# Gated attention with a token and channel mixer: two mirrored key groups in batch 0, and weight loads that wait for the newest square

## The chip, the cores and the metric

The kernel runs on one core of a Trainium2 chip. The metric is the device time of one execution in microseconds (us); several runs are summarised by their median. One execution was also taken with the hardware profiler, and its trace is what the views below are read from. "The span" is the time from the first to the last instruction in that trace.

## The reference

For each of 8 batches, with S = 3008 rows, 256 columns and keys of 64 columns, all inputs in float32:

```python
scores = z @ z.T / S                     # 3008 x 3008, symmetric
attn   = maximum(scores, 0) ** 2
x      = u * (attn @ v)                  # gated attention
h      = maximum(x.T @ w_tok1, 0) @ w_tok2
y      = x + h.T                         # token mixer, 256 tokens wide
out    = y + maximum(y @ w_ch1, 0) @ w_ch2   # channel mixer, 1536 wide
```

The query and the key are the same z, so the score matrix is symmetric: the block of query block q against key group g is the transpose of the block of query block g against key group q.

## The kernel before, in words

**Tiling.** The rows are cut into six query blocks of 512 rows (the last one has 448) and into six key groups of four 128-row tiles (the last group, number 5, ends with a half tile). A block (b, q, g) is batch b, query block q, key group g. It is made in two units: two score matmuls side by side in the two halves of the array's rows (L440), a relu from PSUM into a bfloat16 tile `at` (ScalarE, L478), and a square in place (VectorE, L486). Then PE multiplies the squared block with `v` into the sums `acc` (L677, also in two row halves at once; L593 for the first query block). When all six groups are summed, the result is added up, gated with the transposed `u` (tile `uT`) and kept as `xT`, which a transposing DMA turns into `x_sb` for the mixer.

**Mirrors.** In batches 1 to 7 only blocks with g >= q are computed. A block with g > q is written in a second layout, and when it is squared, a transposing DMA issued on SP (`flip`, its DMA at L546) writes its mirror, block (b, g, q), into a tile `fl`; such an `at` tile has two uses, its own matmuls and the DMA. In batch 0 every block is computed and none is mirrored, because `MIRROR = NQ` makes `direct_block` true for all of them. There are 6 buffers for `at` and 15 for `fl`; the six `v` tiles of batch 0 lie in `fl` buffers too, until the last query block has used them.

**Who decides the order.** All instructions are placed by a planner in the kernel's own code, which runs when the program is built: it keeps an estimated time for PE (`pe[0]`) and for ScalarE, VectorE and SP, and chooses the next piece of work from buffers and results that it estimates to be ready. `key_order` gives the order in which blocks of a query block are made and used; `units` is the list of score units of the whole run. On the chip, each engine works through its list in order and waits on semaphores.

**Loads.** All loads of `v`, `z`, `u` and the weights are issued on GpSimd's queue (POOL), with a cast to bfloat16. In batch 0 they are hung on the count of key groups that PE has begun (`at_group`): the list `items` (L1626) spreads six `v` loads of batch 1, six of `w_tok1`, six of `w_tok2`, four of `w_ch1` and `w_ch2` and two of `u` for batch 1 over groups 7 to 33. That is only an order in POOL's list: no instruction of POOL waits for the group's work, so POOL issues as soon as one of its eight DMA semaphores is free again. From batch 1 on, loads are asked for at least 4 us of planned time apart, and each is preceded by `after(recent[0])` (L121), a copy of one column of the newest square (or of a later stage's newest tile) into a scrap tile `mark`, so that POOL waits for that work.

**SP's queue** holds all transposing DMAs in one order: `uT`, `zT` of the next batch, `x_sb`, `fl`, and `at` blocks on the diagonal, and the stores of the output.

The mixer of a batch is woven into the attention of the next one. That of batch 0 begins after the first query block of batch 1.

Of the kernel before, what the change touches and what calls it, by code (L numbers as in the profile page):

```python
# [57 lines left out]
def kernel(  # L58
# [22 lines left out]
    NQ = (S + QW - 1) // QW  # L81
    NG = KT // GK
# [30 lines left out]
    def rows_of(ap, c):  # L113

        n = full_tiles[c]
        return ap[c * QW:c * QW + n * P, :].rearrange("(p t) d -> p t d", t=n)

    def last_rows(ap):
        return ap[(KT - 1) * P:, :]

    def after(column):  # L121

        nc.gpsimd.tensor_copy(mark[:column.shape[0], :1], column)
# [77 lines left out]
    def load_v(b, c):  # L201
        if b == 0:

            vt = sb.tile([P, GK, D], BF16, tag="fl", name="v_sb", bufs=ROOM["fl"])
            live["fl"] += 1
            fl_free.pop(0)
        else:
            vt = sb.tile([P, GK, D], BF16, tag="v", name="v_sb", bufs=ROOM["v"])
            live["v"] += 1
        n = full_tiles[c]  # L210
        nc.gpsimd.dma_start(out=vt[:, :n, :], in_=rows_of(v[b], c))
        if n < GK:
            for r in range(2):
                nc.gpsimd.dma_start(
                    out=vt[r * TAIL:(r + 1) * TAIL, n, :], in_=last_rows(v[b]))
        vs[b, c] = vt
        v_in[b, c] = Done(pe[0] + 9.0 if b > 1 else 0.0)
        loading(LOAD)
# [20 lines left out]
    def load_w_tok1(c):  # L239
        n = full_tiles[c]  # L240
        nc.gpsimd.dma_start(
            out=w_tok1_sb[:, c * GK:c * GK + n, :], in_=rows_of(moe_w_tok1, c))
        if n < GK:
            nc.gpsimd.memset(w_tok1_sb[TAIL:, KT - 1, :], 0.0)
            nc.gpsimd.dma_start(
                out=w_tok1_sb[:TAIL, KT - 1, :], in_=last_rows(moe_w_tok1))
        loading(LOAD)
# [20 lines left out]

    WHOLE, MIRROR = 1, NQ
    zTs, vs, urs, uTs, xTs, xs = {}, {}, {}, {}, {}, {}
    v_in = {}
    attn = {}

    def direct_block(b, q, g):

        return g >= q or (b == 0 and g < MIRROR)

    def flips(b, q, g):  # L280

        return g > q and not direct_block(b, g, q)
# [3 lines left out]
    def key_order(b, q):  # L286

        direct = [g for g in range(LAST) if direct_block(b, q, g)]
        flipped = [g for g in range(LAST) if not direct_block(b, q, g)]
        first = (b, q) == (0, 0)  # L290
        if first:
            direct = FIRST[:-1]
        made = direct + [LAST] if first else direct[:1] + [LAST] + direct[1:]
        order = []
        while direct or flipped:
            order += direct[:1] + flipped[:1]
            del direct[:1], flipped[:1]
        order.insert(LAST if first else 2, LAST)
        return made, order
# [13 lines left out]
    def loading(us):  # L313
        loads[0] = max(loads[0], pe[0] + 1.0) + us
# [9 lines left out]
    ROOM = {"at": 6, "fl": 15, "xT": 9, "v": NG, "us": 3, "res": RES}  # L324
# [86 lines left out]
    def can_score(first_unit, most):  # L411

        n, at = 0, live["at"]
        for (b, q, g), pr in units[first_unit:first_unit + most]:
            if (b, q) not in turned or (b, g) not in turned:
                break
            at += pr == 0
            if at > ROOM["at"]:
                break
            n += 1  # L420
        return n
# [62 lines left out]
    def square(unit, view, t):  # L484
        (b, q, g), pr = unit
        nc.vector.tensor_mul(view, view, view)  # L486
        if (b, q, g) in early:
            for e in early[b, q, g][2 * pr:2 * pr + 2]:
                e.t = t
            if pr == 0:  # L490
                blocks[b, q, g] = (
                    Done(t), ats[b, q, g].rearrange("p (i w) -> p i w", w=QW), "at", [1])
            else:
                ats.pop((b, q, g))
            return
        if pr < GK // 2 - 1:
            return
        at = ats.pop((b, q, g))
        uses = [1]
        if flips(b, q, g):  # L500
            uses[0] = 2
            attn = at.rearrange("p (j i s) -> p i j s", i=GK, s=P)
            done = push("sp", t, 2.2, 6.5, lambda t: flip(b, q, g, at, uses, done),
                        frees=fl_free,
                        room=lambda: has_room(("fl",)) and flips_fit(b) and (
                            b < 2 or q or
                            x_done[divmod(b * NQ + q - 1, NQ)].t is not None))
        else:
            attn = at.rearrange("p (i w) -> p i w", w=QW)
        blocks[b, q, g] = (Done(t), attn, "at", uses)  # L510
        recent[0] = at[:, :1]
# [24 lines left out]
    def flips_fit(b):  # L536

        n = live["fl"] - live["mix"]
        before_mixer = b < 2 and goal[0] < (0, 0)
        return n < (MIRRORS if before_mixer else AHEAD if in_mixer[0] else ROOM["fl"])  # L540

# [148 lines left out]
    def next_half(t):  # L690

        blk = cur[0]
        if blk is None:
            return FAR, None
        if blk.whole:
            return next_whole(t)
        if blk.g is not None:
            g, dh, tiles = blk.steps[blk.half]
            at = t if blk.acc[dh or 0] is not None else slot_ready(t)
            return max(at, block_ready(blk, g)), g  # L700
        at = t if blk.acc[0] is not None else slot_ready(t)
        return next_group(blk, at)
# [780 lines left out]
    def at_group(n, f):  # L1483
        fetch.setdefault(n, []).append(f)
# [3 lines left out]
    recent = [None]  # L1488
# [131 lines left out]
    W_LATER = 4  # L1620

    def ask_w_tok2(c):
        load_w_tok2(c)
        tok2_done[c].t = pe[0] + 10.0

    items = [lambda c=c: load_v(1, c) for c in vorder]  # L1626
    items += [lambda c=c: load_w_tok1(c) for c in range(NG)]
    items += [lambda c=c: ask_w_tok2(c) for c in range(NG)]
    items += [lambda part=part: ask_w_ch(part) for part in range(4)]
    items += [lambda m=m: load_u(m // NQ, m % NQ) for m in (NQ, NQ + 1)]  # L1630
    for k, item in enumerate(items):
        at_group(NG + 1 + k * (NQ * NG - 2 * NG + W_LATER) // len(items), item)

    fill(7, bank_pair(0, "wp")[:, 0, :])

# [32 lines left out]
    while cur[0] is not None or heads or tails:  # L1668
# [3 lines left out]
        ta, g = next_half(t)  # L1672
# [15 lines left out]
        n = can_score(done_units, most)  # L1688
# [118 lines left out]
```

## Time and profile before

| | us |
|---|---|
| median of 3 runs | 1116.61 (1116.57 to 1119.4) |
| the profiled execution, its own time | 1118.43 |
| its span | 1116.6 |
| PE busy | 1110.1 |
| VectorE busy | 760.8 |
| ScalarE busy | 671.0 |
| GpSimd busy | 152.6 |
| attention of batch 0 after its first query block, by PE's timeline | from 26.9 to 89.9 |
| mixer of batch 0, first matmul of `a_ps` | 101.51 |

The granted clock of TensorE is 1.000 throughout. Busy time is the time in which an engine had an instruction in work; matmuls overlap one another in the array, so their single durations are longer than the step from one to the next. A DMA is shown with the time that its issue took on the queue of its engine, and with the time from issue to landing.

### The profile page before, as it was taken

To read this page: it belongs to the slowest core of one execution; us is meant where nothing else is said; L and a number is where in the kernel's file an instruction comes from. 1 tells how busy PE (TensorE), PEld (TensorE's weight loads), DVE (VectorE), ACT (ScalarE), POOL (GpSimd) and SP (SyncE) were. 2 spreads that over 40 slices of the span, in tenths; PEclk is the share of its full clock that TensorE was granted. 3 is DMA by queue.
4 is the path that set the end of the run, shared out by engine and by line. 5 is a ranking of instruction groups with operands and counts; after the bars stand their busy time and mean duration, and the time that the engine had idled before them with its cause. 6 is when DMAs were issued, how large, how long until landed. Compare 5 with 4: busy or idle time off the path is not lost.

```text
span 1116.6 us, 26566 instructions
## 1 busy us (share of the span) xinstructions
PE 1110.1 (99%) x10788; PEld 672.0 (60%) x10788; DVE 760.8 (68%) x1593; ACT 671.0 (60%) x846; POOL 152.6 (14%) x387
## 2 busy tenths in 40 slices
PE   9999999999999999999999999999999999999998
PEld 3555655666447665676545765567654576545776
DVE  6887766676756867568666676566756677655676
ACT  7996676545755467555665456664666636743464
POOL 5401100221002210022100221003210021000000
PEclk9999999999999999999999999999999999999999
DMA  9999587998849988599795997869888697574222
GB/s 177 184 167 156 123 168 132 179 182 149 165 111 191 173 134 172 107 204 168 146 170 104 204 152 151 171 101 217 143 150 162 121 202 145 119 153 81 68 64 80
DMA packets 473004, 165.98 MB, mean 149 GB/s; under 512 B 435824, under 2 KB 451504, under 8 KB 472880
## 3 DMA queue, kind: packets, MB, share of 16 engines
q1 hardware_dynamic: 445024, 131.57, 60.3%
q0 software_dynamic: 27344, 32.32, 20.9%
q8 instruction: 84, 1.38, 0.6%
q10 hardware_dynamic: 512, 0.38, 0.1%
q14 instruction: 40, 0.33, 0.1%
HBM read 65.40 MB, written 24.64 MB: 81 GB/s over the span
## 4 chain that ended last, share of the span: by engine, by line
PE 99%; DMA 0%; DVE 0%; SPq 0%; issue 0%
PE acc L677 42%; PE hp L977 22%; PE f L1096 18%; PE sc L440 7%; PE a_ps L900 4%; PE h_ps L927 4%; PE f L1209 1%; PE first_acc L593 1%; PE op L1255 0%; DMA zf<-in_z_dram 0%; PE first_acc L198 0%; PE zp L177 0%; DVE zr L171 0%; PE up L1589 0%; DVE res L1287 0%; SPq L162 0%
## 5 line engine op out<-in xcount | busy, mean ns | idle before, releaser
L1024 ACT ACTIVATE h2pre<-hp 128x1024 bf16<-128x1024 f32 (+1 forms) x287 | 283.3, 1005 | 226.6 <-PE hp L977 218.1
L677 PEld LDWEIGHTS <-v_sb 64*128 64x128 bf16 x4418 | 235.4, 94 | 223.1 <-issue 1.1
L677 PE MATMUL acc<-at,v_sb 64*128 64x512 bf16 (+1 forms) x2738 | 337.3, 374 | 0.0
L478 ACT ACTIVATE at<-sc 128x1024 bf16<-128x1024 f32 (+1 forms) x284 | 279.7, 1029 | 72.3 <-PE sc L440 66.9
L977 PE MATMUL hp<-xT,w_ch_sb 128*128 128x512 bf16 (+1 forms) x1152 | 281.7, 375 | 0.0
L486 DVE TENSOR_TENSOR at<-at 128x1024 bf16<-128x1024 bf16 (+1 forms) x284 | 194.0, 687 | 122.3 <-ACT at L478 120.4
L1096 PEld LDWEIGHTS <-h2pre 128*128 128x128 bf16 x3654 | 225.0, 98 | 55.3 <-issue 2.6
L677 PE MATMUL acc<-fl,v_sb 64*128 64x512 bf16 (+1 forms) x1680 | 192.2, 367 | 0.0
L1096 PE MATMUL f<-w_sums,h2pre 128*128 128x128 bf16 x2088 | 184.4, 219 | 0.0
L977 PEld LDWEIGHTS <-w_ch_sb 128*128 128x128 bf16 x1152 | 104.3, 98 | 82.1 <-issue 0.8
L440 PE MATMUL sc<-zT 64*128 64x512 bf16 (+1 forms) x732 | 132.3, 360 | 0.0
L1096 PE MATMUL f<-w_ch_sb,h2pre 128*128 128x128 bf16 x1566 | 128.5, 219 | 0.0
L811 DVE TENSOR_TENSOR cp<-acc,cp 128x512 f32<-128x512 f32 (+1 forms) x94 | 63.5, 676 | 59.9 <-ACT cp L805 59.1
L805 ACT COPY cp<-acc 128x512 f32<-128x512 f32 (+1 forms) x91 | 53.0, 583 | 81.9 <-PE acc L677 81.4
L466 ACT ACTIVATE at<-sc 128x512 bf16<-128x512 f32 (+3 forms) x164 | 59.1, 452 | 35.5 <-PE sc L440 30.4
L1049 DVE TENSOR_TENSOR h2pre<-h2pre 128x512 bf16<-128x512 bf16 (+1 forms) x141 | 56.3, 400 | 18.7 <-PE f L1096 17.8
L440 PEld LDWEIGHTS <-zT 64*128 64x128 bf16 x732 | 40.2, 94 | 41.5 <-issue 3.8
L1170 DVE TENSOR_TENSOR res<-f,res 128x512 f32<-128x512 f32 (+1 forms) x47 | 30.6, 651 | 49.7 <-PE f L1096 49.7
L1051 DVE TENSOR_TENSOR h2pre<-h2pre 128x512 bf16<-128x512 bf16 (+1 forms) x141 | 57.1, 405 | 9.4 <-DVE h2pre L1050 0.5
L936 DVE TENSOR_TENSOR xT<-xT,h_ps 128x1024 bf16<-128x1024 bf16 (+1 forms) x48 | 55.8, 1171 | 11.2 <-PE h_ps L927 11.2
L835 DVE TENSOR_TENSOR xT<-cp,uT 128x512 bf16<-128x512 f32 (+1 forms) x94 | 62.5, 664 | 1.2
L518 DVE TENSOR_TENSOR at<-at 128x512 bf16<-128x512 bf16 (+3 forms) x164 | 43.9, 320 | 25.0 <-ACT at L466 23.9
(80 smaller groups left out, 623.7 us busy)
## 6 DMA issues: line engine op xcount, KB each, us to landing
out_dram<-res SPq DMA_DIRECT2D x80, 256.0 KB, 2.4
v_sb<-in_v_dram POOLq DMA_DIRECT2D x40, 256.0 KB, 4.8
ur<-in_u_dram POOLq DMA_DIRECT2D x40, 256.0 KB, 5.2
out_dram<-res SPq DMA_DIRECT2D x24, 128.0 KB, 2.0
w_tok_sb<-in_moe_w_tok_dram POOLq DMA_DIRECT2D x10, 256.0 KB, 10.2
zs<-in_z_dram POOLq DMA_DIRECT2D x35, 64.0 KB, 3.9
at<-at SPq DMA_TRANSPOSE x123, 2.4
fl<-at SPq DMA_TRANSPOSE x105, 4.6
```

Source lines behind the costliest of these rows:

```text
L440: nc.tensor.matmul(sc[:, r, c0:c1], zT[h, k:k + P], zT[h, m + c0:m + c1], start=True, stop=True)
L466: nc.scalar.activation(a3[:, i, c0:c1], sc[:, r, c0:c1], ACT.Relu, scale=inv_S)
L478: nc.scalar.activation(view, sv, ACT.Relu, scale=inv_S)
L486: nc.vector.tensor_mul(view, view, view)
L677: nc.tensor.matmul(o, vs[blk.b, g][rows, i, dh * P:(dh + 1) * P], rhs, start=(dh, h) not in blk.begun, stop=stop, skip_group_check=True)
L811: nc.vector.tensor_add(cp[:, :W], acc[:, 0, :W], cp[:, :W])
L835: nc.vector.tensor_mul(xT[:, dh, :full * P].rearrange("p (t s) -> p t s", s=P), acc[:, :full * P].rearrange("p (t s) -> p t s", s=P), uT[: ...
L977: nc.tensor.matmul(hp[:, r, :W], w_ch1_sb[:, dc, cc * P:(cc + 1) * P], xT[:, dc, :W], start=(dc == 0), stop=(dc == DT - 1))
L1024: nc.scalar.activation(h2[:, :, :W], hp[:, :, :W], ACT.Relu)
L1049: (3, lambda: nc.vector.tensor_sub(a11, a11, a21)),
L1051: (2, lambda: nc.vector.tensor_sub(a22, a22, a11)),
L1096: banked(nc.tensor.matmul(to[:, j, :], lhs[:, j * P:(j + 1) * P], rhs, start=m in (1, 2) and c2 == 0 and j == 0, stop=c2 == CHT // 2 - 1, ...
```

## The change

Two things change, both in batch 0. The key groups 3 and 4 of the last query block are no longer computed: blocks (0, 3, 5) and (0, 4, 5) are written in the mirror layout and their mirrors come by DMA. With that, the order in which query block 5 uses its groups goes from 0, 1, 5, 2, 3, 4 to 0, 3, 5, 1, 4, 2, and the order in which it makes them from 0, 5, 1, 2, 3, 4 to 0, 5, 1, 2. And every load of `items` behind the six `v` loads (the 16 loads of weights and the two of `u`) is preceded on POOL by `after(recent[0])`.

```diff
-    WHOLE, MIRROR = 1, NQ
+    WHOLE = 1
+    FLIPPED = ((5, 3), (5, 4))
...
     def direct_block(b, q, g):
 
-        return g >= q or (b == 0 and g < MIRROR)
+        return g >= q or (b == 0 and (q, g) not in FLIPPED)
...
         n = live["fl"] - live["mix"]
+        if b == 0:
+            return n < ROOM["fl"]
         before_mixer = b < 2 and goal[0] < (0, 0)
         return n < (MIRRORS if before_mixer else AHEAD if in_mixer[0] else ROOM["fl"])
...
+    def paced(item):
+        after(recent[0])
+        item()
+
...
     for k, item in enumerate(items):
-        at_group(NG + 1 + k * (NQ * NG - 2 * NG + W_LATER) // len(items), item)
+        at_group(NG + 1 + k * (NQ * NG - 2 * NG + W_LATER) // len(items),
+                 (lambda item=item: paced(item)) if k >= NG else item)
```

## The prediction

> **What bounds the kernel now.** I read the page's busy times and chain first, then PE by stretches of ten microseconds, then PE's timeline around the last query block of batch 0, and last the DMA issues of two short stages.
>
> The page says that PE is busy almost all the time and that the chain of work that ended last consists of PE:
>
> ```profile
> PE 1110.1 (99%) x10788; PEld 672.0 (60%) x10788; DVE 760.8 (68%) x1593; ACT 671.0 (60%) x846; POOL 152.6 (14%) x387
> ...
> PE 99%; DMA 0%; DVE 0%; SPq 0%; issue 0%
> ```
>
> The table by stretches shows the stage that the change touches (columns: stretch, its length, then busy time and count for PE, weight loads, VectorE, ScalarE, POOL, then PE's clock, DMA share, GB/s):
>
> ```profile
> 30.00:40.00 10.00, 10.00 (x96) 5.35 (x94) 7.86 (x12) 10.00 (x12) 4.41 (x10) 1.00 1.21 198
> 70.00:80.00 10.00, 10.00 (x102) 5.57 (x98) 8.38 (x15) 8.97 (x12) 0.75 (x2) 1.00 1.27 137
> 80.00:90.00 10.00, 10.00 (x106) 6.02 (x104) 7.58 (x13) 9.31 (x12) 0.00 (x0) 1.00 0.60 119
> ```
>
> PE has no gap there. Busy time alone would not prove it, as single matmuls overlap, so I check the step from one instruction to the next in PE's timeline (start, length, line, what, count). It also shows the work that the change removes:
>
> ```profile
> 77.67 0.37 PE L440 MATMUL sc<-zT 64*128 64x448 bf16 x2
> 77.86 0.94 PE L677 MATMUL acc<-at,v_sb 64*128 64x448 bf16 x8
> 78.61 0.37 PE L440 MATMUL sc<-zT 64*128 64x448 bf16 x2
> 78.80 1.69 PE L677 MATMUL acc<-at,v_sb 64*128 64x448 bf16 x16
> ```
>
> Eight matmuls, four pairs, take 78.61 - 77.86 = 0.75 us, 0.19 a pair, and a score pair the same 0.19 (77.67 to 77.86); the pairs follow each other at one step whatever they belong to. So the time is the sum of PE's steps: a removed pair is worth its step, and everything else counts only when it makes PE wait.
>
> The Trainium skill ("Trainium Kernel Development and Optimization", Performance Expectations) calls matmul busy time a bad metric for the distance to the limit and wants the use of the array counted. Had only the 99% been there, the gain could be anything from nothing to the whole sum; the constant step agrees with the full sum, so I keep it.
>
> **What the change removes from PE.** Blocks (0,5,3) and (0,5,4) have two score units each, so 4 pairs of 448 columns: 4 x 0.19 = 0.76 us. Their matmuls with `v` stay, now read from `fl`; the groups have the same mean there as from `at` at full width (367 ns against 374 on the page), so no change. ScalarE loses 4 relus and VectorE 4 squares, worth nothing because PE does not wait for either in this stage.
>
> **What it adds on SP.** Two transposes of an `at` tile, 128 x 2048 values of 2 bytes = 0.52 MB each. They have much time before block 5 uses them: (0,3,5) is squared at 49.0, (0,4,5) at 61.8, and query block 5 starts on PE at 77.86. The tighter limit is the `at` buffer: six buffers go round, so the sixth block after it writes the same one. Counting two score pairs a block back from the first 448-wide pair at 69.47, block (0,3,5) has its scores at 45.72 and 46.59, block (0,4,5) at 58.46 and 59.32, block (0,5,5) at 71.14. VectorE's timeline gives the squares of the second units:
>
> ```profile
> 48.34 0.69 DVE L486 TENSOR_TENSOR at<-at 128x1024 bf16<-128x1024 bf16 x1 [0.23 <-ACT at L478]
> ...
> 61.07 0.69 DVE L486 TENSOR_TENSOR at<-at 128x1024 bf16<-128x1024 bf16 x1 [0.22 <-ACT at L478]
> ```
>
> They end at 49.03 and 61.76. ScalarE starts a relu about 0.6 us after its scores (0.45 for block 5), so the buffers are written again at 59.07 and 71.59. **Each mirror has some 10.0 and 9.8 us to land**; what lands later delays a relu, then a PSUM bank, then PE.
>
> How long does a mirror take? The two stages of the trace of before lie far apart. While POOL's loads run (27 to 53 us; size, then median us from issue to landing):
>
> ```profile
> w_tok_sb<-in_moe_w_tok_dram POOLq DMA_DIRECT2D x10, 256.0 KB, 10.2
> w_ch_sb<-in_moe_w_ch_dram POOLq DMA_DIRECT2D x4, 384.0 KB, 15.0
> ...
> zT<-zs SPq DMA_TRANSPOSE x3, 20.6
> ...
> x_sb<-xT SPq DMA_TRANSPOSE x1, 17.2
> uT<-ur SPq DMA_TRANSPOSE x1, 18.9
> ```
>
> and when none runs (87 to 94 us):
>
> ```profile
> fl<-at SPq DMA_TRANSPOSE x2, 4.3
> ...
> x_sb<-xT SPq DMA_TRANSPOSE x1, 3.0
> ```
>
> So the lower end is 4.3 us, the upper 17.2 to 20.6. Which one holds depends on the other half of the change.
>
> **What the waits do.** In before, POOL issues the weights as fast as its semaphores allow:
>
> ```profile
> 28.72 1.60 POOL L241 DMA_DIRECT2D w_tok_sb<-in_moe_w_tok_dram  x3
> ...
> 51.46 0.83 POOL L263 DMA_DIRECT2D w_ch_sb<-in_moe_w_ch_dram  x1 [0.74 <-DMA w_tok_sb<-in_moe_w_tok_dram]
> ```
>
> The first lands at about 28.7 + 10.2 = 38.9, the last at 51.5 + 15.0 = 66.5. With the waits, item k goes to group 7 + 28k/24, so the 16 weight loads to groups 14 to 31. Groups take (77.86 - 26.90) / 24 = 2.12 us (PE's timeline: query block 1 starts at 26.90, block 5 at 77.86). That is 44 to 80 us. POOL's issues at 33.91, 35.33 and 36.82 each waited for one of the last loads of `v` and `u`; so from 36.8 to 44 no load would run, and SP can catch up: the `zT` transposes, which held it until 62.7 in before, have room ahead of the first mirror.
>
> In before the loads from 37 to 66.5 take 29 us for 17 items (one of them `u`), 1.7 us each; 16 x 1.7 = 27 us of the 38 from 44 to 82, a share of 0.71. A transpose moves 0.61 MB in 26 us beside loads (the queue totals for 27 to 53 us), 0.023 MB/us, and about 0.28 MB/us alone (GB/s row of 87 to 94). The mean is 0.29 x 0.28 + 0.71 x 0.023 = 0.098 MB/us, so a mirror needs 5.4 us, plus 4.3 - 0.52/0.28 = 2.4 fixed: **an estimate of 7.8 us, under the 9.8 it has**. I take no stall, and keep 4.3 and 20.6 as ends. In SP's queue only `uT` and `x_sb` (0.26 MB each) can stand ahead of a mirror.
>
> What else stands behind a waiting mark on POOL: the loads of `u` block 5 (now about 55, turned about 62, needed for the gate after 90), `u` of batch 1 (about 82 to 85, landing 5.2 us later by the page; turned at 88.5 and 95.65 in before), and a memset. Who waits for the weights: `w_tok1`, issued by 55, is used at 101.51; `w_tok2` by 70, at 106.96; `w_ch`, issued by 80 to 82 and landing 15.0 later at most, 97, is summed by VectorE at 96.31 in before and used by PE at 109.57. The cover is 12 us on PE; without it each microsecond late is one lost.
>
> The 18 marks take 0.18 us each on POOL (the median of the rows at L123), 3.3 us in all. In before, 8 squares overlap a mark and take 0.690 us on average, as the 202 others do, and VectorE idles 1.6 to 2.4 us in each ten of the table above: I take nothing; without that cover they would cost VectorE their 3.3 us.
>
> The Trainium skill ("SBUF — State Buffer", Who interferes with whom) speaks against them: a VectorE instruction with two SBUF inputs and a GpSimd instruction that reads SBUF lock each other out of a port. By it the marks could hold VectorE for as long as they last; the squares of this trace show no such loss.
>
> **The sum.** 1118.43 - 0.76 = 1117.67 for the profiled execution, whose time stands 1.82 above the median; the span 1116.6 - 0.76 = 1115.8. For the median: 1116.61 - 0.76 = **1115.85 us**, -0.07%. A measurement of this kernel can tell about 0.3% from no change, 3.35 us; this lies inside.
>
> **Rivals.**
>
> First, **the mirrors land late** (slower). They wait in SP's queue, or loads come in clumps: groups 16 and 17, 18 and 19, 22 and 23 are begun together. For: the 17.2 to 20.6 above. Against: the loads are spread. It decides from 10.0 us on; past 0.76 us of lateness in total the change loses, past 4.1 us by over 0.3%. At 17.2 each: (17.2 - 10.0) + (17.2 - 9.8) = 14.6, 1130.4 us; at 12 each 4.2, 1120.0. Chance 0.16: half of it a small loss up to 4.1 us (up to 1119.9), half above.
>
> Second, **the weights come too late** for the mixer: needs 12 us beyond 97; if `w_ch` took 30 us, 3 us, 1118.9. Chance 0.03, 0.01 of it above the bound.
>
> Third, **the waits don't spread the loads**, because the newest square in POOL's list is already done when POOL gets there. Then the mirrors fall under the first rival, with 17.2: 1130.4. Chance 0.02.
>
> Fourth, **the planner's order shifts** after block 5: batch 1 starts four units earlier, and the 0.2 us that PE loses at 90.8 (the score pair at 90.77 is followed after 0.4 instead of 0.22) may go or others come: 1115.3 to 1117. Chance 0.07.
>
> Fifth, **ScalarE bounded the stage after all** (10.00 of 10 in 30:40): then 4 relus of 0.93 us (the 128x896 form) go, 3.7 us, 1112.9. PE's even step speaks against it. Chance 0.02.
>
> **How the numbers follow.** The forecast has 0.70. Faster by over 0.3%: 0.02. Slower: 0.08 + 0.01 + 0.02 = 0.11. Within: 0.87. The range goes from 1115.3, the lower end of the fourth rival, to 1118.6, which takes in the smaller stalls (up to 2.7 us over the forecast); what lies outside is the 0.11 above the bound, the upper part of the small stalls and the fifth rival, some 0.17.
>
> **What would show it.** Right: 8 score matmuls at L440 fewer; `fl` transposes 105 + 2; landings of `zT` and `x_sb` in 27 to 53 us down from 17 to 20 to under 8; PE 10.00 in each ten from 30 to 90. Wrong: ScalarE waiting for a DMA at 59 or 72, with PE below 10.00 there, or PE waiting before `a_ps`, `h_ps` or `hp` of batch 0 for a weight.

## The result, and the profile after

| | before | after |
|---|---|---|
| median of 6 runs each, us | 1116.66 (1115.78 to 1119.4) | 1131.2 (1128.93 to 1142.24) |
| the profiled execution, us | 1118.43, span 1116.6 | 1131.22, span 1129.4 |

The ratio is 1.0136, 95% interval 1.0111 to 1.0161: slower by 14.5 us. The forecast was 1115.85; the first rival (mirrors land late) had named 1130.4. In all comparisons below, single runs that stand over 1.5% above the fastest run of the same kernel are left out of the ratio; where that matters, all times are listed.

The page of after answers to the lines shown of before: busy times, the chain that ended last, the score matmuls, and TensorE's clock in 40 slices of 28 us.

```profile
PE 1110.7 (98%) x10780; PEld 672.1 (60%) x10780; DVE 759.2 (67%) x1589; ACT 667.6 (59%) x842; POOL 157.6 (14%) x405
...
PEclk9979999999999999999999999999999999999999
...
PE 97%; DMA 3%; DVE 0%; ACT 0%; issue 0%; ACTq 0%
...
L441 PE MATMUL sc<-zT 64*128 64x512 bf16 (+1 forms) x724 | 130.3, 359 | 12.2 <-ACT at L479 12.2
```

The work went as the diff says: 8 score matmuls fewer (724, before 732), 4 relus and 4 squares fewer. But DMA now stands in the chain with 3%, the score matmuls carry 12.2 us of idle time, and the third slice has a lower clock. The table by stretches finds the place (PE, weight loads, VectorE, ScalarE, POOL, PE's clock, DMA share, GB/s):

```profile
50.00:60.00 10.00, 9.62 (x90) 5.09 (x87) 7.80 (x13) 7.98 (x9) 4.39 (x10) 1.00 1.27 139
60.00:70.00 10.00, 0.00 (x0) 0.00 (x0) 0.00 (x0) 0.00 (x0) 0.00 (x0) 0.69 1.45 91
70.00:80.00 10.00, 8.17 (x52) 3.61 (x53) 5.81 (x10) 6.06 (x7) 1.70 (x4) 0.63 1.01 173
80.00:90.00 10.00, 10.00 (x98) 5.38 (x96) 7.88 (x14) 8.93 (x11) 4.82 (x10) 1.00 0.74 113
```

For ten microseconds nothing computes at all; only the DMA engines are busy. The chain of work between 40 and 80 us (start, length, what) says which transfer that is:

```profile
47.10 0.75 PE acc L680 x7
47.85 22.82 DMA fl<-at
...
70.75 1.03 ACT at L479
...
71.83 0.61 PE sc L441 x2
```

It is the first new mirror, issued on SP at 47.85. It lands 22.8 us later, at 70.67, and 0.08 us after that ScalarE begins the relu that writes the same `at` buffer again. ScalarE had been ready since 70.75 - 12.35 = 58.40, as its own timeline shows (the bracket is the idle time and what ended it):

```profile
70.75 2.85 ACT L479 ACTIVATE at<-sc 128x1024 bf16<-128x1024 f32 x3 [12.35 <-DMA fl<-at]
```

So the mirror had 58.40 - 47.85 = 10.55 us from its issue and took 22.8. (The prediction's 10.0 us count from the end of the block's second square. VectorE's timeline has that square at 45.66 for 0.69 us here, so counted like this the mirror had 58.40 - 46.35 = 12.05.) PE stopped when its PSUM banks were full, and came back at half speed:

```profile
59.01 0.61 PE L680 MATMUL acc<-at,v_sb 64*128 64x512 bf16 x4
71.83 0.61 PE L441 MATMUL sc<-zT 64*128 64x512 bf16 x2 [12.21 <-ACT at L479]
72.21 1.94 PE L680 MATMUL acc<-at,v_sb 64*128 64x512 bf16 x8
73.92 0.66 PE L441 MATMUL sc<-zT 64*128 64x512 bf16 x2
74.34 3.44 PE L680 MATMUL acc<-at,v_sb 64*128 64x512 bf16 x16
77.61 0.39 PE L441 MATMUL sc<-zT 64*128 64x512 bf16 x2
```

From 72.21 to 73.92 four pairs of 512 columns take 1.71, 0.43 each; from 77.61 on (0.39 for two that overlap, the next group at 77.82) the step is 0.21 again. From 71.83 to 77.61 fourteen pairs take 5.78 us where 14 x 0.215 = 3.0 would do: 2.8 us lost behind the pause.

**Where the time went.** The spans differ by 12.8 us. From the first `acc` matmul to the first `a_ps` after had 88.79 us and before 74.61, 14.18 more; the parts are 12.4 of pause (59.24, start of the last pair, to 71.83, less one step) + 2.8 of slow steps - 0.76 of removed pairs = 14.4. The profiled execution of before had begun its first `acc` matmul 2.69 us later (26.90 against 24.21); PE's list is the same in both up to there, so this is not counted to the change. From the first `a_ps` of batch 0 to that of batch 1 after has 1.09 more; 1.0 of it is a wait of PE for an `at` transpose that took 5.9 us beside a load of `u` (182 to 188 us). The rest differs by 0.2.

**What ran beside the mirror.** DMA issues of after in 47 to 49 us (size, median us to landing):

```profile
w_tok_sb<-in_moe_w_tok_dram POOLq DMA_DIRECT2D x1, 256.0 KB, 9.9
w_tok_sb<-in_moe_w_tok_dram POOLq DMA_DIRECT2D x1, 192.0 KB, 10.3
uT<-ur SPq DMA_TRANSPOSE x1, 11.5
fl<-at SPq DMA_TRANSPOSE x1, 22.8
```

and the DMA engines in the ten microseconds of standstill, with packets, megabytes and share of the 16 engines for SP's transposes (q1) and POOL's loads (q0):

```profile
GB/s 42 79 59 57 43 56 51 40 72 52 43 57 52 52 48 61 53 49 42 58 71 71 147 138 140 89 124 113 122 129 114 159 156 182 193 157 168 113 102 83
DMA packets 1827, 0.91 MB, mean 91 GB/s; under 512 B 1228, under 2 KB 1827, under 8 KB 1827
...
q1 hardware_dynamic: 1197, 0.30, 84.5%
q0 software_dynamic: 630, 0.61, 60.5%
```

The crowded stage of before shows how slow this is. There both kinds of traffic ran together too (27 to 53 us):

```profile
DMA packets 5605, 4.91 MB, mean 189 GB/s; under 512 B 2780, under 2 KB 4321, under 8 KB 5601
...
q0 software_dynamic: 3147, 4.26, 96.5%
q1 hardware_dynamic: 2454, 0.61, 18.8%
```

That is 164 GB/s of loads and 23 of transposes. In the standstill both together move 91, and 53 in its first five microseconds. Loads with hardly a transpose beside them moved 192 (81 to 83 us of the fifth experiment), transposes alone 280 to 290. A transposing packet carries 0.30 MB / 1197 = 250 bytes. On average it took 0.845 x 160 us / 1197 = 113 ns in the standstill, 0.188 x 416 / 2454 = 32 ns in the crowded stage of before, and 18 ns where no load runs (the fences of the fifth experiment below: 0.783 x 24 / 1068). So this is not the crowded stage of before again, but a worse one.

### The profile page after: what moved, and what is told of

Same layout as the page of the kernel before. It is cut to its first block, busy times and chain, and to the rows that moved or that the text cites. A ratio compares the mean times of both kernels' runs of the same rounds, so it can differ in the third digit from the quotient of the medians.

```text
span 1129.4 us, 26576 instructions
## 1 busy us (share of the span) xinstructions
PE 1110.7 (98%) x10780; PEld 672.1 (60%) x10780; DVE 759.2 (67%) x1589; ACT 667.6 (59%) x842; POOL 157.6 (14%) x405
## 4 chain that ended last, share of the span: by engine, by line
PE 97%; DMA 3%; DVE 0%; ACT 0%; issue 0%; ACTq 0%
PE acc L680 40%; PE hp L980 22%; PE f L1099 18%; PE sc L441 6%; PE a_ps L903 4%; PE h_ps L930 4%; DMA fl<-at 2%; PE f L1212 1%; PE first_acc L596 1%; DMA at<-at 1%; PE op L1258 0%; PE wp L198 0%; DVE cp L814 0%; PE first_acc L198 0%; ACT at L479 0%
## 5 line engine op out<-in xcount | busy, mean ns | idle before, releaser
L479 ACT ACTIVATE at<-sc 128x1024 bf16<-128x1024 f32 (+1 forms) x280 | 275.7, 1031 | 83.1 <-PE sc L441 64.8
L487 DVE TENSOR_TENSOR at<-at 128x1024 bf16<-128x1024 bf16 (+1 forms) x280 | 191.5, 688 | 133.2 <-ACT at L479 130.6
L680 PE MATMUL acc<-fl,v_sb 64*128 64x512 bf16 (+1 forms) x1712 | 196.3, 367 | 0.0
L441 PE MATMUL sc<-zT 64*128 64x512 bf16 (+1 forms) x724 | 130.3, 359 | 12.2 <-ACT at L479 12.2
L123 POOL CAST mark<-at 128x1 f32<-128x1 bf16 x30 | 8.8, 293 | 438.2 <-DVE at L487 438.2
L939 DVE TENSOR_TENSOR xT<-xT,h_ps 128x1024 bf16<-128x1024 bf16 (+1 forms) x48 | 55.8, 1171 | 11.5 <-PE h_ps L930 11.5
```

Of the source, the lines that this page charges most:

```text
L441: nc.tensor.matmul(sc[:, r, c0:c1], zT[h, k:k + P], zT[h, m + c0:m + c1], start=True, stop=True)
L479: nc.scalar.activation(view, sv, ACT.Relu, scale=inv_S)
L680: nc.tensor.matmul(o, vs[blk.b, g][rows, i, dh * P:(dh + 1) * P], rhs, start=(dh, h) not in blk.begun, stop=stop, skip_group_check=True)
```

## The experiments

The theory after this result: a mirror lands late because weight loads are in flight beside it, and the two kinds of traffic slow each other. The rivals: SP's queue holds it up, the buffer count alone decides, the waits themselves hold something, or the cost lies in another part of the change than the mirrors. Line numbers of `kernel.py` shift by a few where lines were added.

### One part alone

**The waits without the mirrors.**

```diff
-    FLIPPED = ((5, 3), (5, 4))
+    FLIPPED = ()
```

> The waits on the newest square stay, no block is mirrored (the list of mirrored pairs is empty). Theory (the loss is a mirror that lands too late while loads run, and holds its at buffer): no mirror, no stall; PE's step unbroken from 30 to 90 us, 1116.6 us within 1; uT and x_sb still land in 10 to 17 us between 44 and 70 us, since the loads still run there. Rival (the waits themselves or the later weights cost the time): over 1120 us, with PE waiting before 110 us.

Measured: 1131.09, 1117.16, 1135.31, 1116.84, 1134.56, 1116.82 us, before 1116.93 beside it; ratio 1.0023 (0.9976 to 1.0069). Batch 0 has no pause, as the theory says. But three of six runs took 14 to 18 us more, and the one of them that was profiled shows why: the waits moved the tail of the loads from 66.5 us to about 100, under the first mirror of batch 1. In before that mirror was issued at 87.09 and landed in 4.3. Its landing, and the waits between 80 and 112 us (total, times, longest):

```profile
fl<-at SPq DMA_TRANSPOSE x1, 19.7
```

```profile
ACT at L479 <- DMA fl<-at: 12.8, 1, 12.8
...
PE sc L441 <- ACT at L479: 11.5, 1, 11.5
```

So half of the runs meet the theory's time; the other half meet the rival's, over 1120 us, and the profiled one also its PE wait before 110 us. The later weights can cost the time by themselves. The wait is again one for a mirror that lands beside loads, but it is a mirror that the change does not touch.

**The mirrors without the waits.**

```diff
-                 (lambda item=item: paced(item)) if k >= NG else item)
+                 item)
```

> The two mirrors stay, the weight loads do not wait. Theory: block (0,3,5)'s mirror is squared at 49 us in the middle of the loads, stands behind zT on SP and lands after 65 us or later, so ScalarE and PE wait over 6 us for the at buffer, (0,4,5) adds some: 1122 to 1145 us. Rival (the waits cost the time): no stall, 1115.9 us.

Measured: 1134.92, 1132.45, 1133.14, 1150.83; ratio 1.0139 (1.0108 to 1.017). Here SP is still busy with `zT` until 62.7, so the first mirror is issued only at 71.19. By then the loads are all but done and it lands quickly, but it is 18.0 us late. Landing (71 to 73 us), and waits (60 to 110 us):

```profile
fl<-at SPq DMA_TRANSPOSE x1, 4.8
```

```profile
ACT at L479 <- DMA fl<-at: 18.0, 1, 18.0
PE sc L441 <- ACT at L479: 17.8, 1, 17.8
```

So the mirrors cost this much with or without waits, in two ways: with loads in the DMA engines, the transposes ahead of the mirror hold SP and delay its issue, or the mirror itself lands late.

**One mirror at a time, waits kept.** `FLIPPED = ((5, 4),)`, then `FLIPPED = ((5, 3),)`.

> The waits stay, only key group 4 of the last query block is mirrored (its mirror landed in 6.7 us in the changed kernel, but behind a stall in which POOL issued nothing). Theory: without that stall it is squared at about 62 us beside the loads of w_tok2 and lands in 12 to 20 us against 9.8 allowed: a stall of 2 to 10 us, 1118 to 1127 us. Rival (only the first mirror has a problem, because it stands behind uT on SP): lands under 8 us, no stall, 1116.2 us.

Measured: 1145.13, 1144.2, 1116.14, 1116.17, all outside the 1118 to 1127 of the theory. The profiled run is the first: the mirror, issued at 63.75 behind a `uT` beside `w_tok2` and `w_ch`, needs 34.9 us (DMA issues of 63 to 65 us):

```profile
uT<-ur SPq DMA_TRANSPOSE x1, 16.6
fl<-at SPq DMA_TRANSPOSE x1, 34.9
```

The two short runs stand 0.8 below the median beside them (1116.93), where one mirror should save 2 pairs x 0.19 = 0.4; the scatter of before (1116.07 to 1117 for most runs) covers the difference. They were not profiled, but a mirror that is late by more than its cover would show in their time. So the same order of loads can leave a mirror in time, or cost 28 us.

> The waits as in the change, only key group 3 mirrored. Theory (the first mirror is squared in the middle of the w_tok1 loads and lands some 22 us after its issue): a stall of about 12 us near 59 us as in the changed kernel, and some 2 us of lower clock behind it: 1129 to 1133 us. Rival (the loss needs both mirrors): 1116.4 us.

Measured: 1125.24, 1136.87, 1126.23, 1128.34; ratio 1.011 (1.0071 to 1.015). The mirror, issued at 46.6, lands in 18.7, and ScalarE waits 6.8, about half of the 12 us that were expected. Each mirror alone suffices for a pause, at its own place.

### Mirrors in a quiet stretch

Both mirrors and the same bytes, but the first twelve loads go early and unpaced (groups 13 to 18 for `w_tok1`), then one wait, and the rest from group 25 on, behind both mirrors.

```diff
+    held = [25, 25, 26, 26, 27, 27, 28, 28, 29, 30, 32, 33]
...
+        at_group(NG + 1 + k if k < 2 * NG else held[k - 2 * NG],
+                 (lambda item=item: paced(item)) if k == 2 * NG else item)
```

> Both mirrors stay; w_tok1 is loaded without waits right behind v (groups 13 to 18, so that POOL issues it from about 29 us), and w_tok2, w_ch and the two u wait once, for the newest square at group 25 (about 66 us), then run freely. So no load should be in flight from about 45 to 66 us, when both mirrors are made. Theory: both mirrors land in 4 to 8 us, no stall, 1115.9 us (0.76 under before). Rival (a mirror of 0.52 MB is slow in batch 0 whatever the loads do, or waits behind other transposes on SP): landing over 10 us, 1119 us or more.

Measured: 1119.3 to 1123.99, median 1121.54; ratio 1.0033 (1.001 to 1.0056). Both mirrors are quick, without any pause in batch 0. The first (54.5 to 56 us) with its stage, then the second (59.5 to 61):

```profile
DMA packets 1068, 0.26 MB, mean 176 GB/s; under 512 B 1068, under 2 KB 1068, under 8 KB 1068
...
q1 hardware_dynamic: 1068, 0.26, 78.3%
...
fl<-at SPq DMA_TRANSPOSE x1, 3.8
```

```profile
fl<-at SPq DMA_TRANSPOSE x1, 5.3
```

This is the direct test: 3.8 and 5.3 us with no load beside, 22.8 with. The landings are the theory's; the time is not (1115.9 was expected). What is left of the loss has moved to batch 1. Its first mirror, issued at 81.74, meets the loads that now run from 62 to 88 and lands in 12.2; waits between 40 and 115 us:

```profile
ACT at L479 <- DMA fl<-at: 8.0, 1, 8.0
...
PE sc L441 <- ACT at L479: 5.1, 1, 5.1
```

### A longer deadline

Seven `at` buffers instead of six, one `fl` buffer less.

```diff
-    ROOM = {"at": 6, "fl": 15, "xT": 9, "v": NG, "us": 3, "res": RES}
+    ROOM = {"at": 7, "fl": 14, "xT": 9, "v": NG, "us": 3, "res": RES}
```

> The changed kernel with 7 at buffers instead of 6 and 14 fl buffers instead of 15. Theory (the loss is the wait for the at buffer that the mirror still reads): the buffer is written again one block, 2.1 us, later, so the stall shrinks from 12.2 to about 10 us: 1128 to 1130 us, and ScalarE's wait for the mirror falls on block (0,4,1) instead of (0,4,5). Rival (PE waits for the mirrored block itself, or for something behind it): the stall stays at 12 us or more, 1131 us.

Measured: 1126.09 to 1134.1, median 1129.79; ratio 1.0117 (1.009 to 1.0145). ScalarE does two more relus, one block, before it stops, so the place of the wait follows the buffer, as the theory says (its timeline):

```profile
52.46 6.68 ACT L479 ACTIVATE at<-sc 128x1024 bf16<-128x1024 f32 x7
75.66 2.85 ACT L479 ACTIVATE at<-sc 128x1024 bf16<-128x1024 f32 x3 [16.52 <-DMA fl<-at]
```

Its size did not shrink as expected: this mirror took 27.2 us instead of 22.8, more than the extra block gave. The relu that waits is the 13th after the mirrored block's own two with six buffers and the 15th with seven (counted in ScalarE's trace), so each buffer is written again one block later than a plain round of six or seven would have it. One buffer more is no remedy for a landing that varies by more than a block.

### One mirror, with the loads held away from it

**Only (5,3):** nine items unpaced at groups 7 to 15 (six `v`, three `w_tok1`), one wait at group 20, and the rest behind it.

```diff
+    FLIPPED = ((5, 3),)
...
+    held = [20, 20, 20, 21, 21, 22, 22, 23, 23, 24, 24, 25, 25, 32, 33]
...
+        at_group(NG + 1 + k if k < 9 else held[k - 9],
+                 (lambda item=item: paced(item)) if k in (9,) else item)
```

> One mirror only, key group 3 of the last query block. Three pieces of w_tok1 are loaded without waits behind v (issued from about 29 us), the other 13 weight loads and two of u wait once, for the newest square at group 20 (about 53 us), then run freely. No load should be in flight from about 42 to 53 us, when block (0,3,5) is mirrored, nor after about 80 us, when batch 1's first mirror comes. Theory (a mirror is slow only while loads are in flight): it lands in 4 to 7 us, no stall, 0.38 us under before: 1116.4 us. Rival (a mirror in batch 0 is late for another reason): landing over 10 us, 1118 us or more.

Measured: median 1122.6 of 12 (1117.37 to 1150.44); ratio 1.005 (1.0029 to 1.0071). The profiled run is the shortest of them (1117.37): the mirror lands in 3.7 and batch 0 has no pause. What the other runs lost was not profiled; their loads run to about 84 us, close to batch 1's first mirror, but that is only argued.

**Only (5,4):** nine weight loads unpaced up to group 21, one wait at group 25, the rest behind it.

```diff
+    FLIPPED = ((5, 4),)
...
+    held = [25, 25, 25, 26, 26, 27, 27, 32, 33]
...
+        at_group(NG + 1 + k if k < 15 else held[k - 15],
+                 (lambda item=item: paced(item)) if k in (15,) else item)
```

> One mirror only, key group 4 of the last query block. Nine weight loads run without waits behind v (from about 29 us to 52), the other seven and two of u wait once, for the newest square at group 25 (about 66 us). SP, held up by the early loads, should have caught up when block (0,4,5) is squared at about 61 us. Theory: the mirror lands in 4 to 9 us, against 9.8 allowed, no stall, 1116.4 us. Rival: SP's queue is still behind, the mirror is issued after 65 us and lands over 10 us late, 1118 us or more; batch 1's first mirror may be hit if the last loads run past 82 us.

Measured: 1115.26 to 1118.14 in nine runs, 1136.4, 1137.81 and 1147.85 in three; median of all 12 1116.59, before 1116.72; ratio 0.9993 (0.998 to 1.0005). This is the best version tried, and it cannot be told from before. The profiled run is the longest: `uT` and `zT` took 18 to 22 us beside the early loads, so SP reached the mirror only at 94.50, and ScalarE waited 27.2 us (waits of 40 to 130 us):

```profile
ACT at L479 <- DMA fl<-at: 27.2, 1, 27.2
PE sc L441 <- ACT at L479: 26.6, 1, 26.6
```

**Both mirrors, loads in three bursts** (five weight loads early, a wait at group 20 before the next four, another at group 25 before the rest).

```diff
+    held = [20, 20, 20, 20, 25, 25, 25, 26, 26, 27, 27, 32, 33]
...
+        at_group(NG + 1 + k if k < 11 else held[k - 11],
+                 (lambda item=item: paced(item)) if k in (11, 15) else item)
```

> Both mirrors. Five weight loads run without waits behind v, four wait for the newest square at group 20 (about 53 us), seven and two of u for that at group 25 (about 66 us), so that no load should be in flight when the two mirrors are made (47 to 53 and 61 to 66 us) nor after about 82 us, when batch 1's first mirror comes. Theory: three landings under 8 us, no stall, 1115.9 us. Rival (the gaps are too short: loads stretch when transposes run beside them, as in the kernel that held all but w_tok1 until 62 us): one of the three lands after 10 us and costs 2 to 12 us, 1118 to 1128 us.

Measured: 1121.92 to 1132.62, median 1128.73; ratio 1.0107 (1.0079 to 1.0135). In the profiled run (1123.18) the mirrors land in 7.4 and 13.6, with two PE pauses of 4.6 us together, as the rival said. It looks as if the gaps between bursts are too short for two mirrors and the `uT` and `x_sb` between them; the longer runs were not profiled.

### Shorter load packets

How do loads slow a transpose? In the slowest microseconds of 60 to 65 a transposing packet took 100 to 119 ns, near the 96 ns that a load packet of 1024 bytes takes in most stages (medians of the trace's packet records); in the run with (5,4) alone, from 76 to 79 us, it took 260 ns beside load packets of 3072 bytes that took 247. It looked as if each transposing packet waits for one load packet. The Trainium skill ("DMA: Bandwidth & Descriptors", Queues, rings and completion order) says that each DMA engine goes round the queues that have work, a packet at a time, where a packet holds several descriptors. The traces agree in part. From 27 to 53 us of before there were 2454 packets of transposes to 3147 of loads, not far from one to one; from 60 to 65 of after, 696 to 93. And in that stretch of before a transposing packet took 31 ns (median) beside load packets of 1024 to 2048 bytes that took 96 to 172, so its own time does not follow the length of the load's. The idea is thus not shown for the slow stage. If it holds, shorter load packets should help. In after, the loads of `w_tok1`, `w_tok2` and `w_ch1` were cut so that their packets are 512 bytes; the bytes are the same.

```diff
-        nc.gpsimd.dma_start(
-            out=w_tok1_sb[:, c * GK:c * GK + n, :], in_=rows_of(moe_w_tok1, c))
+        for t in range(n):
+            nc.gpsimd.dma_start(
+                out=w_tok1_sb[:, c * GK + t, :], in_=rows_of(moe_w_tok1, c)[:, t, :])
...
+        for h0 in range(c * QW, c * QW + widths[c], QW // 2):
+            cols = slice(h0, min(h0 + QW // 2, S))
...
+            for c0 in range(0, d_ch, D):
```

> The changed kernel, with the loads of w_tok1, w_tok2 and w_ch1 cut into DMAs whose packets have 512 bytes in SBUF instead of 2048, 1024 and 3072; same data, same waits, more DMAs. In the changed kernel a transpose's 256-byte packet takes 18 ns in quiet and, while both kinds run thinly, some 100 to 260 ns, about the time of one load packet. Theory (a transpose's packets wait behind single load packets): with packets a quarter as long the first mirror lands in 8 to 14 us instead of 22.8, the stall shrinks below 5 us: 1118 to 1123 us. Rival (what counts is how long loads are in flight at all): smaller packets move fewer bytes per us, the landing stays at 20 us or more, 1130 us or more.

Measured: 1122.89 to 1129.52, median 1125.9; ratio 1.0083 (1.0058 to 1.0107). DMA of 46 to 52 us:

```profile
q1 hardware_dynamic: 1733, 0.44, 76.1%
q0 software_dynamic: 920, 0.42, 61.7%
...
w_tok_sb<-in_moe_w_tok_dram POOLq DMA_DIRECT2D x9, 64.0 KB, 5.1
fl<-at SPq DMA_TRANSPOSE x1, 7.4
```

A transposing packet takes 0.761 x 96 / 1733 = 42 ns here. The first mirror lands in 7.4 instead of 22.8, and its pause is gone. The median lies between what theory and rival gave. The second, issued at 62.98 beside `w_tok2` with equally short packets, still needs 15.0 and makes PE wait 6.3 us.

**The quiet schedule with short packets**, for `w_ch1` and the three `u` loads near batch 1's first mirror:

```diff
+        if (b, q) in ((0, 5), (1, 0), (1, 1)):
+            for t in range(n):
+                nc.gpsimd.dma_start(out=ur[:, t, :], in_=rows_of(u[b], q)[:, t, :])
```

> The kernel that held w_tok2, w_ch and u until about 62 us (both mirrors landed in 3.8 and 5.3 us there, but batch 1's first mirror took 12.2 beside w_ch and u and cost 5.2 us), now with w_ch1 and the u loads behind it in packets of 512 bytes. Theory (a transpose waits behind single load packets, so short ones cost it less): batch 1's first mirror lands in under 10 us, no stall, 1116 us. Rival (the loads themselves are in its way, whatever their packets): its landing stays at 12 us or more, 1120 to 1123 us.

Measured: median 1120.24 of 12 (1118.69 to 1132.33); ratio 1.0041 (1.0017 to 1.0064). Batch 1's first mirror lands in 12.2 as before the cut; PE waits 1.7 us for it instead of 5.1. On the landing, the rival held, and the pause still shrank.

**Only (5,3), waits as in the change, with short packets** (the load cuts of the last two together):

> Only key group 3 mirrored, waits as in the change, w_tok1, w_tok2, w_ch1 and the three u loads behind the waits in packets of 512 bytes. With long packets this mirror landed in 18.7 us and the kernel took 1127.28 us. Theory: it lands in about 7 us as it did with short packets and both mirrors, and batch 1's first mirror under 10, so no stall: 1116.4 us. Rival (the short landing was chance): over 10 us, a stall of 5 us or more, 1121 to 1130 us.

Measured: 1124.07 to 1132.04, median 1127.15; ratio 1.0094 (1.0063 to 1.0124). The mirror lands in 8.9 where long packets gave 18.7, and batch 0 has no pause: the effect of the shorter packets on this stage is repeated. But the median is that of (5,3) alone with long packets, 1127.28: batch 1's first mirror lands in 13.3 beside loads of `u`, and costs about what was won (waits of 80 to 115 us):

```profile
ACT at L487 <- DMA fl<-at: 7.8, 1, 7.8
...
PE sc L449 <- ACT at L487: 6.6, 1, 6.6
```

## Why the prediction was wrong, point by point

**PE's sum fits what was measured.** 8 score matmuls are gone, and their step is 0.19 us here too (86.54 to 86.73 on PE's timeline). Where one mirror lands in time, the time stands a fraction of a microsecond under before: 1116.14 and 1116.17 with (5,4) alone, and 1116.0 as the median of the nine shorter runs of its held version, against 1116.72. That is within the scatter of before (1115.77 to 1117.75 for most runs). The 0.76 us itself was not seen, as every version with both mirrors lost time elsewhere.

**The deadline was of the right kind, but 2.0 us too tight.** The `at` buffer decides: ScalarE starts 0.08 us after the landing, and one buffer more moves the wait by a block. The prediction took the sixth block after the mirrored one for the next writer of its buffer, 10.0 us after the square; it is the seventh, 12.05 us after it. A likely reason, not tested, is that block (0,3,5) is made second in its query block but used third, so that its buffer comes free one block later. As SP reached the mirror 1.5 us after the square, 10.55 us were left, and the two errors nearly cancel.

**SP's catching up was right, its consequence too small.** The last `zT` left SP's queue at 43 instead of 62.7, and the first mirror was issued at 47.85, ahead of its need. But the `uT` in front of it took 11.5 us to land, on the same slow engines. The prediction had named `uT` and `x_sb` as all that could stand ahead of a mirror, and priced them at nothing.

**The step that failed is the landing, "an estimate of 7.8 us, under the 9.8 it has".** It measured 22.8, even above the upper end of 20.6. The term that was mis-sized is the mean rate of 0.098 MB a microsecond. These are the totals of 48 to 60 us of after; those of 60 to 70 are above:

```profile
q0 software_dynamic: 874, 1.24, 70.1%
q1 hardware_dynamic: 2328, 0.58, 53.8%
```

All transposes together moved 0.58 + 0.30 = 0.88 MB in these 22 us, 0.040 MB a microsecond, and at most 0.52 of it was the mirror; the rest was other transposes, the `uT` in front and the `x_sb` behind among them. Three things were wrong.

- *The mean over time.* It gave a mirror the crowded rate of 0.023 for a share of 0.71 and the quiet rate of 0.28 for 0.29, as if loads kept their own length and left gaps. In 48 to 60 us the loads' packets hold 70.1% and the transposes' 53.8% of the engines' span, which leaves hardly any gap. The three `w_tok2` loads issued in 50 to 60 us took 14.1 us to land (median), where the table for 27 to 53 of before has 10.2 for the same size. Transposes moved 0.048 MB a microsecond from 48 to 60 and 0.030 from 60 to 70, both far nearer the crowded rate.
- *The mirror alone.* The estimate gave the whole rate to the mirror, though other transposes were in flight with it.
- *The spacing of the loads.* "2.12 us a group" is a mean. After its first three pieces of `w_tok1` POOL issued the other four transfers of `w_tok1`, and a `u`, from 44.8 to 50.8, close around the mirror's issue. The prediction named such clumps in its first rival and left them out of the mean.

The table sets the main profiled landings side by side (0.52 MB each):

| mirror | issued | landed after, us | beside it |
|---|---|---|---|
| first or only, after | 47.85 | 22.8 | `w_tok1`, `u`, `w_tok2` |
| (5,3) alone, paced | 46.6 | 18.7 | the same |
| both, seven buffers | 48.4 | 27.2 | the same |
| after with 512-byte packets | 46.89 | 7.4 | the same, cut |
| quiet schedule | 54.97, 60.04 | 3.8, 5.3 | no load |
| (5,3) alone, held | 51.44 | 3.7 | no load |
| second mirror, after | 70.86 | 6.7 | the last `w_tok2` in flight, then none, as the pause held POOL |
| after with 512-byte packets, second | 62.98 | 15.0 | `w_tok2`, cut |
| batch 1's first, quiet schedule | 81.74 | 12.2 | `w_ch`, `u` |
| batch 1's first, after | 95.95 | 9.6 | `w_ch`, `u` |
| (5,4) alone, paced, a long run | 63.75 | 34.9 | `w_tok2`, `w_ch` |
| batch 1's first, waits alone | 84.36 | 19.7 | `w_ch`, `u` |
| batch 1's first, before | 87.09 | 4.3 | no load |

No mirror without a load beside it took over 5.3 us. Beside loads the landings spread widely: 18.7 to 34.9 us for the first mirror of batch 0 among paced, uncut loads, but 9.6 for batch 1's first in after, where loads were in flight too. That the loads are the cause is shown by the quiet schedule, and by (5,3) alone paced against held (18.7 and 3.7), which differ only in when the loads run and in how many marks POOL makes; the run without waits shows that the marks are not needed for the loss.

**The first rival was right, with too small a chance.** It named the cause, and "at 17.2 each" it said 1130.4 us, 0.8 from the median. That it is so near is luck: the first mirror was 12.3 us late instead of 7.2, the second not at all instead of 7.4, because the pause stopped POOL's marks and with them the loads, and 2.8 us of slow steps, which it did not have, made up the rest. The 17 to 20 us of transposes in before came from the same mix of traffic, so its row was the nearest one; the mean with the quiet row had no instance in the trace. There was one that spoke against it: in 68 to 75 us of before, with little more than one `u` load beside `uT` and `x_sb`, all of them together moved only 97 GB/s, with 9.5 us for a `uT` that takes 2.8 alone. Nobody waited for it there, so it did not show in any wait.

**Weights not late: right for the mixer, but the question was too narrow.** No mixer matmul of batch 0 waited for a weight. What the later loads hit was batch 1's first mirror, whose deadline the prediction did not list among those who stand behind a moved load; by itself this cost 11.5 us of PE in the profiled run with waits alone, and three of its six runs took 14 to 18 us more.

**The marks** cost VectorE nothing, as forecast: in after, the 25 squares that overlap a mark took 0.68 us on average and the 255 others 0.69. No wait of PE shows the planner's order or ScalarE's own work as a part of the loss.

**What stays open.** Loads beside a mirror are needed for a late landing, but they do not always bring one. Why it differs so much from run to run of one kernel (the waits alone, (5,4) alone) is not settled; no run tells what the two outcomes start from. Nor is the mechanism inside the DMA engines: shorter packets helped the first mirror (22.8 to 7.4, 18.7 to 8.9), but hardly the `w_tok2` stage (15.0) and not batch 1's first mirror (12.2 both ways). No version tried beats before by more than a measurement can tell.

## What to carry to other kernels

A transfer's landing must be priced under the traffic that will run beside it, from a stage of the trace with that mix; a mean of a crowded and a quiet row is no such price, as the two streams together moved 53 GB/s for five microseconds here, where loads alone moved 192 and transposes alone 280 to 290. The other transfers of the same queue belong in that price. The first deadline of a mirrored block is the reuse of its source buffer, not the use of its result. A load that is moved later lands on something: list every transfer that was quiet there before, those of other batches too.

## What the runs showed of the hardware that was not expected

- Loads from POOL's queue and transposes from SP's, in flight together, did not have one rate. They moved 189 GB/s from 27 to 53 us of before (164 and 23), and 53 from 60 to 65 of after. The profiled run of the held (5,4) version shows both within one stretch: 147 to 204 GB/s from 40 to 50 us, then 33 to 96 up to 62. A transposing packet of 250 bytes took 18 ns with no load beside it, 32 in that stretch of before and 113 from 60 to 70 of after (means). What decides between the two is open.
- After a pause of 12.2 us PE works at a step of 0.43 instead of 0.21 us for 5.8 us, 2.8 us lost; the granted clock is 0.69 from 60 to 70 us and 0.63 from 70 to 80. The Trainium skill ("TensorE: Matmul & The Clock Gate", Part 1) says that the array's clock is halved after an idle window of some 3.4 us and comes back after a busy one; the halved step agrees, and 5.8 us lie between one and two such windows. The price of this pause is thus its own length and 2.8 us. Five other profiled pauses of 7 to 28 us were followed by 3.3 to 5.0 us of the slow step, and lost 1.6 to 2.4 us by the same count.
